# Attention, gated MLP and soft mixture in one kernel: h of three batches turned on VectorE, probabilities of two batches divided on GpSimd

## The chip, the cores and the metric

One core of a Trainium2 chip runs the whole program. The metric is device microseconds of one execution, and the median of three runs is 853.25 us (852.73 to 855.25). The profiled execution took 852.55 us.

## The reference

```
q_n = q / sqrt(mean(q*q) + 1e-6) * g_q           # k the same; 4 batches, 12 heads, 448 tokens, 64 wide
p   = exp(s - max(s)),  s = q_n @ k_n.T / 8
x   = (p / (sum(p) + 1e-9)) @ v                  # 1792 tokens x 768
h   = silu(x @ w_gate) * (x @ w_val)             # 1792 x 1536
y   = h @ w_out
logits = y @ phi                                 # 1792 x 32 slots
d = softmax of logits over all tokens;  slot_in = d.T @ y
8 experts, 4 slots each: slot_out = relu(slot_in @ w1) @ w2
out = softmax of logits over the slots @ slot_out
```

Everything is f32. `y` is never formed: the kernel uses `w_out @ phi` for the logits and `(d.T @ h) @ w_out` for the slots' input.

## The kernel before

The order of every engine's instructions is written out by hand. The program is a row of steps `t`; in each, a list of two-letter items is called one after the other, and every engine works its own instructions off in that order. `ORD1` (line 1244) is the list while the first batch's MLP runs, `ORD2` (line 1247) the list after it. Step `u = t - 28` does one 128-row half of the MLP: even `u` the gate, odd `u` the value of one block of 128 hidden units (`gv`, 18 matmuls in two halves `G0` and `G1`). A batch takes 24 steps, so batch b runs in steps 24b to 24b+23, and there are 96.

Attention runs ahead of the MLP in the same steps, one block of 112 queries for a pair of heads per step, four steps (c = 0 to 3) to a pair, pairs 7 to 23 in steps u = 0 to 67; from step 68 on there is no attention left. For each step: `S` scores on TensorE, `M0` and `M1` the row maxima on VectorE (line 473), `E0` and `E1` the exponentials with their row sums on ScalarE (line 483), `P0` and `P1` the transposes of the step before's probabilities on TensorE (line 519), `V0` and `V1` their evacuation. Once in a pair come `T` (transposes of the next pair's q in c = 0, k in c = 1), `TH` and `L` (their split in high and low parts on ScalarE and VectorE, lines 404, 434, 62, 446), `X` (probabilities times v, c = 1, line 547) and `XH`, `XL` (the split of the result, lines 59 and 62).

The division by the row sums is done once for a pair, after `X`. `NA` (line 491 on ScalarE, 492 on VectorE, 494 on GpSimd) inverts the sums and spreads them over a 112 x 512 tile, `NB` turns that tile on TensorE (line 504), `NC` evacuates it (line 511), and `XM` (line 575) multiplies.

`h` comes out of the MLP with hidden units on partitions. `AT` (tanh, line 621) and `AM` (lines 628 and 634 on VectorE) finish it, `LG` multiplies it with `w_out @ phi` for the logits (every 8 steps, in the last batch every 4, line 668). `HT` turns it to tokens on partitions: four TensorE transposes of 128 x 112 into one PSUM bank (line 647) and one ScalarE copy into `hn` (line 648), every second step. The slots' part of a batch is done in the first steps of the next: `Z1` and `Z2` in step 1, `Z3` and `Z4` in step 2, where `Z4` (line 735) reads the batch's three `hn` tiles. The pool of `hn` has three buffers.

`WH` and `WL` split the next step's weights (line 231 on ScalarE, 239 on VectorE); in the last batch `W4` does it. `G0` of the next step needs both. Short transposes and sums share the three PSUM banks of tag `t`. `Q` is the normalisation of later q and k on GpSimd (lines 340, 341 and 347).

Of the kernel before, what the change touches and what calls it, by code (L numbers as in the profile page):

```python
# [8 lines left out]
F32 = mybir.dt.float32  # L9
# [6 lines left out]
ALU = mybir.AluOpType  # L16
# [5 lines left out]
def attn_moe_softmoe_kernel(  # L22
# [33 lines left out]
    EPS_SUM = 1e-9  # L56
# [28 lines left out]
    ident = cpool.tile([P, P], F32, name="ident")  # L85
# [69 lines left out]
    NU = 2 * KF  # L155
# [126 lines left out]
    NPR = len(pairs)  # L282
    NT_ = NPR * NC
    st = {}
    xt = {}
# [191 lines left out]
    def sexp(t, j):  # L477
# [7 lines left out]
        )  # L485
        d["pr"][j] = p

    def sums_inv(i):

        su = st[i]["su"].rearrange("p c j -> p (c j)")  # L490
        nc.scalar.activation(out=su, in_=su, func=AF.Copy, bias=EPS_SUM)
        nc.vector.reciprocal(out=su, in_=su)  # L492
        rs = ap_.tile([P, 2 * NC * HD], F32, tag="rs", name="rs", bufs=1)
        nc.gpsimd.tensor_copy(  # L494
            out=rs[:CP].rearrange("p (n d) -> p n d", d=HD), in_=su.unsqueeze(2).to_broadcast([CP, 2 * NC, HD])
        )
        st[i]["rs"] = rs
# [26 lines left out]
    def pevac(t, j):  # L524
        i, c = divmod(t, NC)
        if c == 0:
            if i < NP and i % 2:
                pt = hnp.tile([CP, NC, 512], F32, tag="hn", name="pt", bufs=3)[:, :, :S]
            else:
                pt = ap_.tile([CP, NC, S], F32, tag="pt", name="pt", bufs=PTB)  # L530
            st[i].setdefault("pt", {})[j] = pt
        eng = nc.vector.tensor_copy if t < M0 and (t % 4, j) in PVD else nc.scalar.copy
        eng(  # L533
            out=st[i]["pt"][j][:, :, c * CP : (c + 1) * CP],
            in_=st[i][c]["tp", j][:CP, :S].rearrange("p (k q) -> p k q", k=NC),
        )
# [30 lines left out]
    def pv_scale(i):  # L567

        b, hp = pairs[i]
        d = st.pop(i)  # L570
        if b == 3 and hp > 3:
            xf = xfp.tile([P, S], F32, tag=f"xh{hp - 4}", name="xf", bufs=1)
        else:
            xf = d["rs"]
        nc.vector.tensor_tensor(out=xf, in0=d["xp"][:, :S], in1=d["rs"], op=ALU.mult)
        xt[b, hp] = xf
# [3 lines left out]
    bt = {}  # L580
# [49 lines left out]
    def act_val(u):  # L630
# [2 lines left out]
        ht = d["ht"][r // 2]  # L633
        nc.vector.scalar_tensor_tensor(out=ht, in0=ht, scalar=0.5, in1=d[r], op0=ALU.mult, op1=ALU.mult)

    def h_trans(u, ht=None):

        b, r = divmod(u, NU)
        fc = r // 2
        g, f4 = divmod(fc, 4)  # L640
        d = bt[b]
        if f4 == 0:
            d["hn"][g] = hnp.tile([CP, NC, 512], F32, tag="hn", name="hn", bufs=3)
        ht = d["ht"][fc] if ht is None else ht
        th4 = pt_tile("th4")
        for c in range(NC):
            nc.tensor.transpose(th4[:CP, P * c : P * c + P], ht[:, CP * c : CP * c + CP], ident)  # L647
        nc.scalar.copy(  # L648
            out=d["hn"][g][:, :, P * f4 : P * f4 + P], in_=th4[:CP, :].rearrange("p (c f) -> p c f", c=NC)
        )  # L650
# [70 lines left out]
    def slots3(b):  # L721
        d = bt[b]
        dp = pt_tile("dp")
        for c in range(NC):
            nc.tensor.transpose(
                dp[:CP, NS * c : NS * c + NS], d["et"][:NS, CP * c : CP * c + CP], ident[:NS, :NS]
            )
        d["dn"] = mp.tile([CP, NC, NS], F32, tag="dn", name="dn", bufs=1)
        nc.vector.tensor_copy(out=d["dn"], in_=dp[:CP, : NC * NS].rearrange("p (c s) -> p c s", c=NC))

    def slots4_mul(b, g):
        d = bt[b]
        sp = pt_tile("sp")
        for c in range(NC):
            nc.tensor.matmul(
                sp[NS * c : NS * c + NS, :], d["dn"][:, c, :], d["hn"][g][:, c, :], start=True, stop=True
            )
        return sp

# [167 lines left out]
    M0 = NP * NC + 4  # L907
# [150 lines left out]
    def step(t):  # L1058
        if t < M0:
            return step0(t)  # L1060
        i, c = divmod(t, NC)
        u = t - M0
        moe = u < B * NU
        prev = u - 1 if 0 <= u - 1 < B * NU else None
        ub, ur = divmod(u, NU)
        pb = ub - 1
        att = t < NT_
# [155 lines left out]
        def Q_():  # L1223
# [114 lines left out]
    with tc.manual_schedule():  # L1338
# [63 lines left out]
        for u, (e, i, n) in enumerate(eunits):  # L1402
            w = wtile.pop(u)
            if i == 0:
                if n == 0:
                    hacc[e] = s_tile(e % 3)[:, :FQ]
                for c in range(KD2 * n, KD2 * n + KD2):
                    for j in range(4):
# [4 lines left out]
                            start=(c == 0),  # L1413
                            stop=(c == KD - 1),
                        )
                if n == 1:
# [8 lines left out]
                    for t in range(2):  # L1425
                        nc.vector.tensor_copy(
                            out=h1m.rearrange("p (j t) s -> p t j s", t=2)[:, t, :, SPE * e : SPE * e + SPE],
                            in_=ht_[:, P * t : P * t + P].rearrange("p (j s) -> p j s", j=4)[
                                :, :, SPE * e : SPE * e + SPE
                            ],  # L1430
                        )
                    h1s[e] = h1m
            else:
                for kh_ in range(KH2 * n, KH2 * n + KH2) if i == 1 else range(KH):
                    for j in range(4) if i == 1 else (2 * n, 2 * n + 1):
# [4 lines left out]
                            start=(e == 0 and kh_ == 0),  # L1440
                            stop=(e == E - 1 and kh_ == KH - 1),
# [52 lines left out]
```

## Time and profile before

| | |
|---|---|
| median of 3 runs | 853.25 us |
| profiled execution | 852.55 us, of it the span 850.2 us |
| PE busy | 801.2 us (94%), 5504 matmuls |
| DVE busy | 492.1 us (58%), 785 instructions |
| ACT busy | 487.2 us (57%) |
| POOL busy | 270.0 us (32%) |

Busy time is the time in which at least one instruction of the engine ran. Matmuls overlap in the array, so that a matmul's own duration (0.37 us for 448 columns) is longer than the distance from one start to the next (0.20 us); where a step's length is told below, it is by starts. The profile's granted TensorE clock is 1.00, which is the 2.4 GHz level, in all stretches between 124 and 730 us.

### The profile page before, as it was taken

Reading aid. Unit: us, or ns where it says so; the run is one execution under the profiler, and the core shown is the slowest. Engines: PE = TensorE matmul, PEld = TensorE weight load, DVE = VectorE, ACT = ScalarE, POOL = GpSimd, SP = SyncE. Lnnn points to the kernel's source line nnn. Section 1 sums busy time; section 2 is a strip of 40 time slices with the busy share of each in tenths; the row PEclk is TensorE's granted clock in tenths of the full one; section 3 lists DMA queues with packets and bytes.
Section 4 is the critical chain, followed back from the end, with each engine's and each line's share of the span. In section 5 each row is a group of like instructions: output and inputs, shape, how many; then the busy total and the mean of one; then the engine's idle time right before and its main releaser. Section 6 shows DMA issues by size and latency. Waiting matters only on the chain.

```text
span 850.2 us, 14278 instructions
## 1 busy us (share of the span) xinstructions
PE 801.2 (94%) x5504; PEld 612.8 (72%) x5504; DVE 492.1 (58%) x785; ACT 487.2 (57%) x1054; POOL 270.0 (32%) x211
## 2 busy tenths in 40 slices
PE   6899989999999999999999999999999999988685
PEld 5566657878877767788778678877888888655343
DVE  4899888889888556565646655554354434221013
ACT  4777877889877746676667467664532323211012
POOL 7977748676777023113330230200000000010000
PEclk8999999999999999999999999999999999999877
DMA  7666655576564322322132122221227888799997
GB/s 212 201 178 205 205 179 185 178 248 198 186 196 152 108 60 66 107 89 89 51 94 89 49 78 67 86 67 57 59 77 239 294 293 319 271 383 403 403 350 235
DMA packets 77891, 148.87 MB, mean 175 GB/s; under 512 B 5888, under 2 KB 48128, under 8 KB 77824
## 3 DMA queue, kind: packets, MB, share of 16 engines
q1 hardware_dynamic: 77824, 147.97, 52.5%
q8 instruction: 43, 0.70, 0.3%
q14 instruction: 24, 0.20, 0.1%
HBM read 128.29 MB, written 19.66 MB: 174 GB/s over the span
## 4 chain that ended last, share of the span: by engine, by line
PE 76%; DVE 8%; DMA 7%; POOL 3%; ACT 3%; issue 2%; SPq 0%; POOLq 0%; ACTq 0%; DVEq 0%
PE pg L607 36%; PE tp L519 7%; PE xp L547 6%; DMA w<-in_moe_w_dram 6%; PE s L466 3%; PE s L468 3%; PE th L647 2%; PE tq L372 2%; DVE sm L473 2%; PE s L547 2%; DVE qa L434 2%; PE so L1436 2%; PE s L463 2%; PE lp L668 2%; POOL rs L494 2%
## 5 line engine op out<-in xcount | busy, mean ns | idle before, releaser
L607 PE MATMUL pg<-xh,wh 128*128 128x448 f32 x576 | 219.6, 381 | 0.0
L607 PE MATMUL pg<-xl,wh 128*128 128x448 f32 x576 | 210.3, 365 | 0.0
L607 PE MATMUL pg<-xh,wl 128*128 128x448 f32 x432 | 158.1, 366 | 0.7 <-DVE wl L239 0.7
L473 DVE TENSOR_REDUCE sm<-s 112x1 f32<-112x448 f32 x192 | 110.7, 618 | 66.6 <-PE s L468 65.3
L483 ACT ACTIVATE pr<-s,sm 112x448 f32<-112x448 f32 x192 | 121.1, 635 | 37.5 <-DVE sm L473 36.3
L494 POOL COPY rs<-su 112x512 f32<-112x512 f32 x24 | 35.6, 1484 | 275.1 <-DVE su L492 268.2
L607 PEld LDWEIGHTS pg<-xh,wh 128*128 128x128 f32 x576 | 108.4, 188 | 17.9 <-issue 10.2
L607 PEld LDWEIGHTS pg<-xl,wh 128*128 128x128 f32 x576 | 108.6, 189 | 7.0
L519 PE MATMUL tp<-ident,pr 112*112 112x112 f32 x768 | 99.6, 261 | 3.0 <-ACT wot L253 1.1
L519 PEld LDWEIGHTS tp<-ident,pr 112*112 112x112 f32 x768 | 82.2, 134 | 17.9 <-issue 2.1
L231 ACT CAST wh<-raw 128x768 fp32r<-128x768 f32 x96 | 79.7, 831 | 25.2 <-PE pg L607 21.8
L533 ACT COPY pt<-tp 112x448 f32<-112x448 f32 x164 | 81.0, 539 | 13.8 <-PE tp L519 7.8
L607 PEld LDWEIGHTS pg<-xh,wl 128*128 128x128 f32 x432 | 81.1, 188 | 8.5 <-DVE wl L239 2.0
L239 DVE TENSOR_TENSOR wl<-raw,wh 128x768 fp32r<-128x768 f32 x72 | 72.7, 1009 | 23.4 <-ACT wh L231 23.1
L341 POOL TENSOR_TENSOR ri<-ss,mhalf 112x16 f32<-112x16 f32 (+1 forms) x25 | 70.2, 2806 | 2.1
L347 POOL TENSOR_TENSOR qn<-qk,ri 112x512 f32<-112x512 f32 x46 | 62.1, 1361 | 2.3
L621 ACT ACTIVATE ht<-pg 128x448 f32<-128x448 f32 x48 | 25.9, 539 | 56.3 <-PE pg L607 56.3
L547 PE MATMUL xp<-pt,vt 112*64 112x448 f32 x288 | 58.1, 545 | 0.0
L648 ACT COPY hn<-th 112x512 f32<-112x512 f32 x48 | 28.4, 592 | 46.6 <-PE th L647 45.2
L607 PE MATMUL pg<-xh,raw 128*128 128x448 f32 x144 | 52.7, 366 | 0.0
L197 POOL TENSOR_SCALAR hpos<-r 128x768 uint16<-128x768 int16 x36 | 44.6, 1239 | 12.2 <-DVE raw L212 8.8
L628 DVE SCALAR_TENSOR_TENSOR ht<-ht,pg 128x448 f32<-128x448 f32 x48 | 29.5, 614 | 31.9 <-ACT ht L621 31.3
(160 smaller groups left out, 1208.7 us busy)
## 6 DMA issues: line engine op xcount, KB each, us to landing
w<-in_moe_w_dram SPq DMA_DIRECT2D x25, 1536.0 KB, 10.3
raw<-w SPq DMA_DIRECT2D x72, 384.0 KB, 3.1
w<-raw SPq DMA_DIRECT2D x36, 384.0 KB, 3.0
r<-in_moe_w_out_dram SPq DMA_DIRECT2D x12, 768.0 KB, 5.2
r<-in_moe_w_gate_dram SPq DMA_DIRECT2D x12, 768.0 KB, 5.7
r<-in_moe_w_val_dram SPq DMA_DIRECT2D x12, 768.0 KB, 5.3
qk<-in_q_dram SPq DMA_DIRECT2D x24, 224.0 KB, 3.4
qk<-in_k_dram SPq DMA_DIRECT2D x24, 224.0 KB, 3.5
```

What stands on the lines that cost most here:

```text
L197: (nc.gpsimd if e == "p" else nc.vector).tensor_scalar(out=o, in0=src, scalar1=-float((0x3800, 0xB800)[j]), scalar2=8.0, op0=ALU.add, op1= ...
L231: (nc.vector.tensor_copy if u - NO < NU and WH1 == "v" else nc.scalar.copy)(out=wh, in_=wst[u]["raw"])
L239: eng.tensor_tensor(out=wl, in0=wst[u]["raw"], in1=wst[u]["wh"].bitcast(F32), op=ALU.subtract)
L341: nc.gpsimd.tensor_tensor(out=ri, in0=ss, in1=mhalf[:, : len(ns)], op=ALU.pow)
L347: eng.tensor_tensor(out=st[i]["qn"][:, n].rearrange("p c h d -> p h c d"), in0=st[i]["qk"][:, n], in1=st[i]["ri"][:, n] .rearrange("p (h c ...
L473: nc.vector.tensor_reduce(out=d["sm"][:, j : j + 1], in_=d["sc"][j], axis=AX.X, op=ALU.max, negate=True)
L483: nc.scalar.activation(out=p, in_=d["sc"][j], func=AF.Exp, bias=d["sm"][:, j : j + 1], accum_out=st[i]["su"][:, c, j : j + 1])
L494: nc.gpsimd.tensor_copy(out=rs[:CP].rearrange("p (n d) -> p n d", d=HD), in_=su.unsqueeze(2).to_broadcast([CP, 2 * NC, HD]))
L519: nc.tensor.transpose(tp[:CP, ck * CP : (ck + 1) * CP], pr[:, ck * CP : (ck + 1) * CP], ident[:CP, :CP])
L533: eng(out=st[i]["pt"][j][:, :, c * CP : (c + 1) * CP], in_=st[i][c]["tp", j][:CP, :S].rearrange("p (k q) -> p k q", k=NC),)
L547: nc.tensor.matmul(xp[HD * j : HD * j + HD, :S], d["vt"][:, j, ck, :], d["pt"][j][:, ck, :], start=(ck == 0), stop=(ck == NC - 1),)
L607: nc.tensor.matmul(d[r], wt[:, P * c : P * c + P], mv, start=(c == 0 and n == 0), stop=(c == KD - 1 and n == 2),)
```

## The change

1. Batches 1 to 3: `HT` is no longer called (but for the very last block). In its place VectorE turns `h` in squares of 32 x 32, sixteen instructions for a block: item `H0` to `H3`, each four instructions over one quarter of the hidden units. A block's `H0` and `H1` stand in the step after it is finished, `H2` and `H3` in the one after that. Tokens then lie in chunks of 128, 128, 128 and 64, and `slots3` and `slots4_mul` follow that.
2. Pairs 12 to 23 (batches 2 and 3): `NA`, `NB`, `NC` and the multiplication in `XM` are gone. `N0` adds the 1e-9 and inverts two sums on VectorE, `N1` and `N2` multiply the two tiles of probabilities in place on GpSimd, in every step, before `P0` and `P1` of the next. `XH` and `XL` read the product from PSUM; two pairs of the last batch get a ScalarE copy.
3. `ORD1` gets the new items, `ORD2` is another order.

```diff
+    def normp(t, part):
+        i, c = divmod(t, NC)
+        su = st[i]["su"][:, c]
+        if part == 0:
+            nc.vector.tensor_scalar(out=su, in0=su, scalar1=EPS_SUM, scalar2=None, op0=ALU.add)
+            nc.vector.reciprocal(out=su, in_=su)
+        else:
+            j = part - 1
+            p = st[i][c]["pr"][j]
+            nc.gpsimd.tensor_scalar(out=p, in0=p, scalar1=su[:, j : j + 1], scalar2=1.0, op0=ALU.mult, op1=ALU.mult)
...
+        if i >= NPX:
+            xt[b, hp] = d["xp"][:, :S]
+            if b == 3 and hp > 3:
...
+                nc.scalar.copy(out=xf, in_=xt[b, hp])
...
+    SQ, WIDE = 32, 1
+    def h_squares(u, g):
+        hn, o = hn_tile(u)
+        hk = hts_[u][SQ * g : SQ * g + SQ]
+        for k in range(P // SQ):
+            m = (S // SQ - k + P // SQ - 1) // (P // SQ)
+            nc.vector.transpose(
+                out=hn[SQ * k : SQ * k + SQ, :m, o + SQ * g : o + SQ * g + SQ],
+                in_=hk.rearrange("p (c q) -> p c q", q=SQ)[:, k :: P // SQ],
+            )
...
-            if c == 0 and NP < i <= NPR:
+            if c == 0 and NP < i <= NPX:
                 sums_inv(i - 1)
...
-                else:
+                elif prev < NU:
                     h_trans(prev)
+        def H_(g):
+            w = prev if g < 2 else u - 2
+            if w is not None and NU <= w < B * NU - 1 and w % 2 == 1:
+                if g == 0:
+                    hts_[w] = bt[w // NU]["ht"][w % NU // 2]
+                h_squares(w, g)
...
     ORD1 = (
-        "SP X NB T S AT W4 NC XM TH XH M1 M0 Z1 P1 Z2 WH AM G0 Z3 P0 E1 XL L NA R0 CT V0 V1 SS WL G1 E0 Q HT Z4 LG R C"
+        "SP X NB T S AT W4 NC XM TH XH M1 M0 Z1 P1 Z2 WH AM G0 Z3 P0 E1 XL L NA R0 CT V0 V1 SS WL G1 E0 N0 N1 N2 Q HT H0 H1 H2 H3 Z4 LG R C"
     ).split()
     ORD2 = (
-        "AT NB X NC T S XM TH XH M0 M1 AM XL E0 E1 SP W4 G0 L NA Z1 Z3 WH P0 V0 P1 V1 Z2 Z4 HT LG SS R0 CT C WL G1 R Q"
+        "NB T TH S X M0 H2 NC NA W4 AT SP XM XH M1 AM SS E0 XL E1 N0 Z3 L P0 G0 Z1 N1 V0 HT H3 WH H0 P1 H1 N2 V1 R0 Z4 CT C WL G1 R Z2 Q LG"
     ).split()
```

## Rows read from the trace of the kernel before

**Rows 1.** The page's part 1: busy us, share of the span, instructions.
```profile
PE 801.2 (94%) x5504; PEld 612.8 (72%) x5504; DVE 492.1 (58%) x785; ACT 487.2 (57%) x1054; POOL 270.0 (32%) x211
```

**Rows 2.** Windows (busy us of PE, PEld, DVE, ACT, POOL): steps 25-47, 48-67, 72-95.
```profile
301.00:461.00 160.00, 156.64 (x932) 128.34 (x931) 93.80 (x150) 107.52 (x235) 36.84 (x27) 1.00 0.26 81
461.00:604.00 143.00, 140.08 (x833) 112.59 (x832) 78.95 (x128) 88.91 (x201) 22.00 (x17) 1.00 0.21 65
624.00:730.00 106.00, 105.62 (x551) 89.12 (x549) 46.03 (x64) 33.44 (x52) 0.29 (x1) 1.00 0.72 253
```

**Rows 3.** Waits of PE from 289 to 604 us: total, times, longest.
```profile
PE th L647 <- DVE qa L434: 4.7, 10, 0.5
```

**Rows 4.** Timeline of PE at a pair's change: start, us, instruction.
```profile
326.25 0.55 PE L519 MATMUL tp<-ident,pr 112*112 112x112 f32 x4
327.27 0.62 PE L647 MATMUL th<-ident,ht 128*112 128x128 f32 x4 [0.47 <-DVE qa L434]
...
329.36 0.36 PE L607 MATMUL pg<-xh,wl 128*128 128x448 f32 x1
329.83 0.60 PE L504 MATMUL rb<-ident,rs 112*128 112x112 f32 x4
330.36 3.23 PE L547 MATMUL xp<-pt,vt 112*64 112x448 f32 x16
```

**Rows 5.** Timeline of PE around one turned block of h, batch 3.
```profile
656.59 0.37 PE L607 MATMUL pg<-xh,raw 128*128 128x448 f32 x1
656.79 0.60 PE L647 MATMUL th<-ident,ht 128*112 128x128 f32 x4
657.15 0.45 PE L607 MATMUL pg<-xh,wh 128*128 128x448 f32 x1
657.43 0.36 PE L607 MATMUL pg<-xl,wh 128*128 128x448 f32 x1
```

**Rows 6.** Timeline of DVE in a step with c = 1.
```profile
334.76 1.16 DVE L473 TENSOR_REDUCE sm<-s 112x1 f32<-112x448 f32 x2 [0.43 <-PE s L468]
...
336.37 0.62 DVE L62 TENSOR_TENSOR xl<-rs,xh 128x448 fp32r<-128x448 f32 x1
336.90 0.61 DVE L62 TENSOR_TENSOR kl<-tq,ka 64x448 fp32r<-64x448 f32 x1
337.53 0.39 DVE L446 CAST ka<-ka 64x448 fp32r<-64x448 f32 x1
337.93 0.63 DVE L62 TENSOR_TENSOR kl<-tq,ka 64x448 fp32r<-64x448 f32 x1
338.58 0.96 DVE L239 TENSOR_TENSOR wl<-raw,wh 128x768 fp32r<-128x768 f32 x1
```

**Rows 7.** Groups of DVE by line and shape, 301 to 604 us: busy, mean ns.
```profile
L575 DVE TENSOR_TENSOR rs<-xp,rs 128x448 f32<-128x448 f32 x10 | 6.2, 625 | 37.8 <-PE xp L547 37.8
...
L492 DVE RECIPROCAL su<-su 112x8 f32<-112x8 f32 x10 | 2.0, 203 | 0.8 <-ACT su L491 0.5
...
L729 DVE COPY dn<-dp 112x128 f32<-112x128 f32 x2 | 0.6, 292 | 1.4 <-PE dp L725 1.4
```

**Rows 8.** Timelines of POOL: the spreading copy twice, and one of batch 0.
```profile
327.49 2.29 POOL L494 COPY rs<-su 112x512 f32<-112x512 f32 x1 [24.73 <-DVE su L492]
...
354.76 0.61 POOL L494 COPY rs<-su 112x512 f32<-112x512 f32 x1 [19.59 <-DVE su L492]
...
256.67 1.67 POOL L197 TENSOR_SCALAR hpos<-r 128x768 uint16<-128x768 int16 x1
```

**Rows 9.** Timeline of DVE beside the last row.
```profile
257.33 1.76 DVE L239 TENSOR_TENSOR wl<-raw,wh 128x768 fp32r<-128x768 f32 x1
```

**Rows 10.** Timelines of DVE and ACT in a step with c = 2.
```profile
340.00 1.16 DVE L473 TENSOR_REDUCE sm<-s 112x1 f32<-112x448 f32 x2 [0.46 <-PE s L468]
341.08 0.61 DVE L634 SCALAR_TENSOR_TENSOR ht<-ht,pg 128x448 f32<-128x448 f32 x1
...
341.81 0.20 ACT L483 ACTIVATION_READ_ACCUMULATOR pr<-s,sm 112x1 f32 x1
```

More of the change, by code (lines that the diff above doesn't have):

```diff
@@ L377, in attn_moe_softmoe_kernel @@
     SPL = 7
+    NPX = 2 * NP
     halves = [slice(0, HD), slice(HD, P)]
@@ L527, in pevac @@
             if i < NP and i % 2:
-                pt = hnp.tile([CP, NC, 512], F32, tag="hn", name="pt", bufs=3)[:, :, :S]
+                pt = hnp.tile([P, NC, 512], F32, tag="hn", name="pt", bufs=3)[:CP, :, :S]
             else:
@@ L570, in pv_scale @@
         d = st.pop(i)
+        if i >= NPX:
+            xt[b, hp] = d["xp"][:, :S]
+            if b == 3 and hp > 3:
+                xf = xfp.tile([P, S], F32, tag=f"xh{hp - 4}", name="xf", bufs=1)
+                nc.scalar.copy(out=xf, in_=xt[b, hp])
+                xt[b, hp] = xf
+            return
         if b == 3 and hp > 3:
@@ L634, in act_val, with tok, hn_tile @@
         nc.vector.scalar_tensor_tensor(out=ht, in0=ht, scalar=0.5, in1=d[r], op0=ALU.mult, op1=ALU.mult)
+    def tok(b):
+        return [P] * (S // P) + [S % P] if b >= WIDE else [CP] * NC
+    def hn_tile(u):
+        b, r = divmod(u, NU)
+        g, f4 = divmod(r // 2, 4)
+        d = bt[b]
+        if g not in d["hn"]:
+            d["hn"][g] = hnp.tile([P, NC, 512], F32, tag="hn", name="hn", bufs=3)
+        return d["hn"][g], P * f4
     def h_trans(u, ht=None):
         b, r = divmod(u, NU)
[L639 to L644, printed above, removed]
-        th4 = pt_tile("th4")
[L646 to L650, printed above, removed]
+        hn, o = hn_tile(u)
+        ht = bt[b]["ht"][r // 2] if ht is None else ht
+        th4 = pt_tile("th4")
+        t0 = 0
+        for c, n in enumerate(tok(b)):
+            nc.tensor.transpose(th4[:n, P * c : P * c + P], ht[:, t0 : t0 + n], ident)
+            t0 += n
+        th4 = th4.rearrange("p (c f) -> p c f", c=NC)
+        n, m = (P, NC - 1) if b >= WIDE else (CP, NC)
+        nc.scalar.copy(out=hn[:n, :m, o : o + P], in_=th4[:n, :m])
+        if b >= WIDE:
+            n = S % P
+            nc.scalar.copy(out=hn[:n, m, o : o + P], in_=th4[:n, m])
+    SQ, WIDE = 32, 1
+    def h_squares(u, g):
+        hn, o = hn_tile(u)
+        hk = hts_[u][SQ * g : SQ * g + SQ]
[5 more added lines that the diff above has]
+            )
+        if g == P // SQ - 1:
+            del hts_[u]
+    hts_ = {}
     def logits(u):
@@ L723, in slots3 @@
         dp = pt_tile("dp")
[L724 to L729, printed above, removed]
+        t0 = 0
+        for c, n in enumerate(tok(b)):
+            nc.tensor.transpose(dp[:n, NS * c : NS * c + NS], d["et"][:NS, t0 : t0 + n], ident[:NS, :NS])
+            t0 += n
+        d["dn"] = mp.tile([P, NC, NS], F32, tag="dn", name="dn", bufs=1)
+        dp = dp.rearrange("p (c s) -> p c s", s=NS)
+        n, m = (P, NC - 1) if b >= WIDE else (CP, NC)
+        nc.vector.tensor_copy(out=d["dn"][:n, :m], in_=dp[:n, :m])
+        if b >= WIDE:
+            n = S % P
+            nc.vector.tensor_copy(out=d["dn"][:n, m], in_=dp[:n, m])
     def slots4_mul(b, g):
@@ L733, in slots4_mul @@
         sp = pt_tile("sp")
-        for c in range(NC):
+        for c, n in enumerate(tok(b)):
             nc.tensor.matmul(
-                sp[NS * c : NS * c + NS, :], d["dn"][:, c, :], d["hn"][g][:, c, :], start=True, stop=True
+                sp[NS * c : NS * c + NS, :], d["dn"][:n, c, :], d["hn"][g][:n, c, :], start=True, stop=True
             )
@@ L1072, in NA @@
         def NA():
-            if c == 0 and NP < i <= NPR:
+            if c == 0 and NP < i <= NPX:
                 sums_inv(i - 1)
         def NB():
-            if c == 1 and NP < i <= NPR:
+            if c == 1 and NP < i <= NPX:
                 sums_spread(i - 1)
         def NC_():
-            if c == 1 and NP < i <= NPR:
+            if c == 1 and NP < i <= NPX:
                 sums_evac(i - 1)
@@ L1172, in E_, with NP_ @@
                 sexp(t, j)
+        def NP_(part):
+            if att and i >= NPX:
+                normp(t, part)
         def P_(j):
@@ L1229, in step @@
             E0=lambda: E_(0), E1=lambda: E_(1), P0=lambda: P_(0), P1=lambda: P_(1), V0=lambda: V_(0), V1=lambda: V_(1),
-            SP=SP, R0=R0, R=R_, CT=CT, C=C_, SS=SS, HT=HT, LG=LG, Q=Q_,
+            N0=lambda: NP_(0), N1=lambda: NP_(1), N2=lambda: NP_(2), SP=SP, R0=R0, R=R_, CT=CT, C=C_, SS=SS,
+            HT=HT, H0=lambda: H_(0), H1=lambda: H_(1), H2=lambda: H_(2), H3=lambda: H_(3), LG=LG, Q=Q_,
         )
```

## The prediction

> **What bounds the kernel now.** The page's busy times come first: PE is busy for 94% of the span, DVE for 58% [rows 1]. The windows then give the stretches that the change touches: from 301 to 604 us (steps 25 to 67, MLP and attention together) PE is busy for 296.7 of 303 us and DVE for 172.8, or 57%; from 624 to 730 us (the last batch, MLP alone) PE for 105.6 of 106 and DVE for 46.0 [rows 2]. So PE sets the pace, and VectorE has 130 and 60 us to spare. What the little idle time of PE hides is read from starts in the timeline: in a step with c = 0 the four transposes of `P1` begin at 326.25, and `th` follows after 1.02 us, where the four of `rb` let the next matmul start after 0.53: 0.5 us late, and the trace calls 0.47 idle, ended by VectorE's split of q, which frees the PSUM bank [rows 4]. PE waits there ten times, 4.7 us [rows 3].
>
> **What TensorE gains.** A turned block of `h` (four transposes) puts `th` 0.36 us ahead of the next matmul, and the one behind it comes 0.28 instead of 0.20 us later [rows 5]: 0.44 us. 35 blocks leave: 15.4 us, of it 9.2 in the 21 of the stretch 301 to 604 and 5.3 in 12 of the last one. `rb` takes 0.53 us to the start of `xp`, and starts 0.27 us late, because GpSimd's copy comes late (matmuls before it go every 0.20 us) [rows 4]. Twelve go, ten of them in 301 to 604: 5.3 us and five late starts, 1.3 us. The ten waits of 0.5 us lose their cause, nine in that stretch: 4.5 us. In 301 to 604 PE then needs 303 - 9.2 - 5.3 - 1.3 - 4.5 = 282.7 us, in the last stretch 106 - 5.3 = 100.7.
>
> **What VectorE pays.** No row shows a VectorE transpose. The nearest row is a copy of 128 elements a partition, 292 ns; the 448-element instruction with 625 ns gives (625 - 292) / 320 = 1.04 ns an element [rows 7], so 259 ns for 96 elements. Whether the next may start early is in rows 6: `xl` and the first `kl` write from partition 0 on, and the second starts 0.53 us after the first, which takes 0.62; from that `kl` to the cast the written block of partitions changes, and 0.63 us pass for an instruction of 0.61. Each of a block's sixteen transposes writes another 32 partitions than the one before, so I count them in full with 15 ns between: 8 x 0.307 + 8 x 0.274 = 4.65 us a block, 0.29 us each. From below: an early start saves 0.08 us each as with `xl`, 0.21 us; from above: two cycles an element, 0.43 and 0.37 us, worked out from the same slope; no row of this kind behaves so, and I take 0.34 us as the end of the range's price. 21 blocks are 97.6 us, 12 are 55.8.
>
> The Trainium skill, VectorE: DVE Perf Modes, section The three transpose paths, speaks against the change: its table has 311 ns for VectorE's 128 x 128 (in 32 x 32 blocks), and its rules send a whole 128 x 128 transpose to TensorE where PSUM will do as its place. No row here shows it. With 19 ns more for each of 560 transposes the sum would be 10.6 us higher, near 852.
>
> `N0` is two instructions on two columns; a reciprocal of 8 columns has 203 ns [rows 7], so 0.4 us at most, in 43 steps 17.2 us. Gone are ten or eleven multiplications `XM` and the reciprocals of eight sums: 6.2 + 0.6 + 2.0 = 8.8 us [rows 7]. In 301 to 604 VectorE then has 172.8 - 8.8 + 97.6 + 17.2 = 278.8 us.
>
> `N0` also waits: the second row sum is read out at 342.01, 2.0 us after the maxima began; VectorE comes there at 341.69 [rows 10]. That is 0.35 us with c = 2, and as much with c = 3, where `H2` delays `M1`; with c = 0 and 1 other work fills it. Over 43 steps 8 us. Queued behind `N0` are `L`, the squares and `WL`, and `G0` of the next step waits for `WL`. `H0` of steps 26, 50 and 74 overwrites an `hn` buffer that `Z4` of the same step still reads, so VectorE stands until TensorE has done `G0` and `P1`: about 1 us each. So 278.8 + 8 + 2 = 289 us for VectorE against 282.7 for TensorE.
>
> **GpSimd.** The spreading copy of 512 elements takes 0.61 us alone and 2.29 us beside VectorE [rows 8]; 448 elements then take 0.5 to 2.0 us, two of them 1 to 4 us. I take 1.6. `N0` ends 2.4 us into a step and `P0` of the next begins over 5 us into it, so neither is late. The other way about costs more: `WL` took 1.76 instead of 0.96 us beside a GpSimd instruction [rows 6, 8, 9]. At most 0.8 us x 43 = 34 us, at least nothing; in a step with c = 2 the multiplications should be over before `WL` starts. I take one `WL` in eleven, 3 us.
>
> **The rest.** ScalarE loses 35 evacuations and twelve `rs` copies and stays under VectorE. `T` ahead of `X` lets `S` and the maxima start 3.2 us earlier with c = 1; `LG` and `Z2` go to the end of the step, where only the next `WL` or the slots wait. No DMA moves. In `ORD1`, `E0` stands behind `V1`, so in steps 21 to 23 the divided tile can come late for `P1`: 0 to 4 us, I take 1.
>
> **The sum.** Two queues so nearly equal, each in its fixed order, hold each other up; I add 3 us for that, the least sure term: 289 + 3 + 3 = 295 instead of 303, 8 us less. Last stretch: VectorE 46.0 + 55.8 + 1 = 102.8, TensorE 100.7; 103.2 with little to spare, 2.8 less. Steps 24 and 68 to 71: 1.2 and 1.4 less. `ORD1` 1 more. 852.55 - 8 - 2.8 - 1.2 - 1.4 + 1 = 840.2, and the median of the runs lies 0.7 us over the profiled one: 841 us. VectorE would be the engine that sets the pace, just ahead of TensorE.
>
> **Rivals.**
> 1. Cheap transposes. At 0.21 us the 560 cost 45 us less, VectorE has slack everywhere and TensorE keeps its gain: 15.4 + 12 x 0.53 + 1.3 + 5.0 = 28.1 us less, 1 more for `ORD1`: 852.55 - 28.1 + 1 + 0.7 = 826 us. For: the maxima and `xl` do start early. Against: the blocks of partitions [rows 6].
> 2. Dear transposes, the slower side. VectorE's queue in steps 26 to 95 decides: each 10 ns on a transpose is 5.6 us, so from 0.312 us on the 12 us are gone. At 0.33 us it is 841 + 22 = 863 us. For: 32 x 32 squares may take time to fill that a copy does not; VectorE has 289 of 295 us filled. Against: nothing but the copy's row.
> 3. No net change: a new wait in place of the one removed. With c = 1, `T`, `X` and `P0` take the three banks, and `P1` needs the one that `L` frees. From the maxima to the end of `L` it is 3.8 us [rows 6], with `H2` (1.2) and `N0` (0.8) 5.8 us; TensorE is at `P1` after `X`, `P0` and `G0`, 3.2 + 0.4 + 1.8 = 5.4 us. If the late VectorE makes that 2.4 us and 1 us of it reaches the next maxima, eleven pairs cost 11 us: 852. That the change does not divide or turn at all can't be; both are written out.
>
> **Chances.** 0.3% of 853.25 is 2.6 us, about what a measurement can tell from no change. Forecast (833 to 849) 0.45; rival 1 (824 to 833) 0.18; rival 3 and the page's price (849 to 856) 0.15, of it 0.02 below 850.7; rival 2 (over 856) 0.22. So faster 0.65, same 0.12, slower 0.23. The range leaves out a little of rival 1 and half of rival 2: 825 to 860; the forecast's own is 833 to 849.
>
> **What would show it.** 560 transposes into `hn` with a mean of 0.26 to 0.29 us and starts 0.29 us apart: right; 0.21 us apart is rival 1, 0.32 rival 2. DVE at about 650 us busy. PE with 188 transposes less, and no `th` waiting for `qa`; `WL` before `G0` as PE's commonest wait, then VectorE sets the pace; `tp` waiting for `kl` is rival 3. `WL` groups with a mean over 1.1 us would show GpSimd in the way, `tp` waiting for GpSimd a division that comes late. If PE has no waits and the time is still 850, the price of its own work was misread.

## The result and the profile after

The changed kernel takes 862.66 us (median of 6 runs, 858.09 to 863.77) against 853.07 us for the kernel before beside it: a ratio of 1.0102, 95% interval 1.0074 to 1.0130. It is 1% slower, where 841 us was forecast. The profiled execution took 858.09 us; the accounting below goes by it and by the 852.55 us of the kernel before.

The busy times, part 1 of the changed kernel's page (busy us, share, instructions), answer to [rows 1]:

```profile
PE 799.7 (93%) x5316; PEld 587.0 (69%) x5316; DVE 657.8 (77%) x1420; ACT 464.8 (54%) x998; POOL 320.6 (37%) x295
```

PE has 188 matmuls less and yet no less busy time; DVE has 166 us more. The windows of the steps of [rows 2] (25 to 47, 48 to 67, and 72 to 95 from 3 us into step 72 on; busy us of PE, PEld, DVE, ACT, POOL):

```profile
303.80:464.20 160.40, 154.60 (x874) 119.71 (x873) 146.94 (x358) 98.04 (x212) 64.38 (x70) 1.00 0.25 78
464.20:606.60 142.40, 138.31 (x762) 102.92 (x762) 127.07 (x319) 81.17 (x180) 43.78 (x53) 1.00 0.22 69
629.30:734.40 105.10, 102.08 (x487) 80.21 (x485) 96.18 (x253) 25.17 (x37) 0.29 (x1) 1.00 0.72 257
```

In the first two VectorE is busy for 274 of 302.8 us, and PE now has idle time. VectorE's dearest groups there, by line and shape (busy us, mean ns, idle before), beside [rows 7]:

```profile
L694 DVE STREAM_TRANSPOSE hn<-ht 32x128 f32<-32x128 f32 x168 | 50.4, 300 | 6.7 <-PE sp L791 3.8
...
L694 DVE STREAM_TRANSPOSE hn<-ht 32x96 f32<-32x96 f32 x168 | 45.6, 271 | 2.3
L239 DVE TENSOR_TENSOR wl<-raw,wh 128x768 fp32r<-128x768 f32 x42 | 40.9, 973 | 1.3
...
L496 DVE RECIPROCAL su<-su 112x2 f32<-112x2 f32 x43 | 7.1, 166 | 1.5
L495 DVE TENSOR_SCALAR su<-su 112x2 f32<-112x2 f32 x43 | 7.0, 164 | 9.8 <-ACT pr L485 9.8
```

The transposes cost 300 and 271 ns, `N0` costs 0.33 us, and `WL` stays at 0.97 us on the mean. The forecast had 292 and 259 ns for the transposes, 0.4 us for `N0`, and a slower `WL` now and then: the prices came out within a few per cent of it, or lower. VectorE's waits in the stretch (total us, times, longest):

```profile
DVE su L495 <- ACT pr L485: 9.8, 26, 1.7
DVE hn L694 <- PE sp L791: 3.8, 2, 2.2
DVE sm L475 <- PE s L470: 3.2, 3, 1.4
DVE xl L62 <- ACT xh L59: 1.7, 1, 1.7
```

The lengths of the steps, from one step's first gate matmul to the next one's, say where the time went (us; "after 95" goes from the last gate matmul's end to ScalarE's last instruction; steps 0 to 19 take 135.7 us in both; the last column is the run e6 below, in which VectorE has little to do):

| steps | before | after | forecast | measured | e6 |
|---|---|---|---|---|---|
| up to 0 | 124.5 | 125.3 | 0 | +0.8 | 125.7 |
| 20 to 23 | 30.0 | 32.6 | +1 | +2.6 | 34.2 |
| 24 | 11.5 | 10.5 | -1.2 | -1.0 | 10.5 |
| 25 to 67 without 49, 50 | 285.6 | 282.5 | -8 with 49, 50 | -3.1 | 265.8 |
| 49, 50 | 17.0 | 20.3 | (in the row above) | +3.3 | 19.0 |
| 68 to 71 | 20.1 | 19.5 | -1.4 | -0.6 | 18.6 |
| 72 to 74 | 18.2 | 22.2 | -2.8 with 75 to 95 | +4.1 | 20.5 |
| 75 to 95 | 87.7 | 86.1 | (in the row above) | -1.6 | 84.7 |
| after 95 | 112.4 | 113.9 | 0 | +1.5 | 113.8 |

The 34.2 us of e6 in steps 20 to 23 hold a stretch at a lower granted clock, 0.79 on the mean from 279 to 287 us, where the kernels before and after have 1.00 (2.4 GHz). Two losses stand out: the slots' steps (49, 50, 73, 74 and the tail), for which the forecast had only VectorE's 1 us at the `hn` buffer, and a gain of 3 instead of 8 us in the long stretch.

Step 50 holds the first of the two. These are the groups of PE by shape while `Z4` runs, in the kernel before (484.6 to 487.5 us) and in the changed one (485.3 to 491.2 us); an f32 matmul leaves two records, so 24 are 12 matmuls:

```profile
L735 PE MATMUL sp<-hn,dn 112*32 112x512 f32 x24 | 2.8, 596 | 0.0
```

```profile
L791 PE MATMUL sp<-hn,dn 128*32 128x512 f32 x18 | 3.2, 604 | 0.0
L791 PE MATMUL sp<-hn,dn 64*32 64x512 f32 x6 | 3.1, 601 | 0.0
```

One record takes as long as before (0.60 us), but before four of them ran beside each other, each in its own 32 columns of the array; the second records of the four followed 0.45 us later, and the next four matmuls 0.88 us after the first. Now the three of 128 rows start together, their second records 0.45 us later, the one of 64 rows 0.53 us after those, its second record 0.45 us later, and the next three 0.52 us after that. It runs beside none of them: four matmuls take 1.96 us instead of 0.88, and the product 5.9 instead of 2.8. The Trainium skill, TensorEngine Tiling (Array Packing), section Key Properties, states this rule: to change the tiling mode, and not just the tile, drains TensorE. By it a 64-row matmul in between costs two drains a group; the trace agrees in that nothing runs beside it, with 1.96 us for four matmuls instead of 0.88. The forecast did not weigh it.

### The profile page after: what moved, and what is told of

The parts are those of the page before. It is cut to its first block, busy times and chain, and to the rows that moved or that the text cites. A ratio compares the mean times of both kernels' runs of the same rounds, so it can differ in the third digit from the quotient of the medians.

```text
span 856.3 us, 14739 instructions
## 1 busy us (share of the span) xinstructions
PE 799.7 (93%) x5316; PEld 587.0 (69%) x5316; DVE 657.8 (77%) x1420; ACT 464.8 (54%) x998; POOL 320.6 (37%) x295
## 5 line engine op out<-in xcount | busy, mean ns | idle before, releaser
L628 PE MATMUL pg<-xh,wh 128*128 128x448 f32 x576 | 223.9, 389 | 1.2 <-DVE ht L649 1.2
L694 DVE STREAM_TRANSPOSE hn<-ht 32x128 f32<-32x128 f32 (+1 forms) x560 | 160.1, 286 | 14.6 <-PE sp L791 5.9
L628 PE MATMUL pg<-xh,wl 128*128 128x448 f32 x432 | 161.0, 373 | 3.8 <-DVE wl L239 3.2
L500 POOL TENSOR_SCALAR pr<-pr,su 112x448 f32<-112x448 f32 x96 | 63.0, 669 | 216.2 <-DVE su L496 101.1
L475 DVE TENSOR_REDUCE sm<-s 112x1 f32<-112x448 f32 x192 | 112.4, 617 | 13.5 <-PE s L470 11.1
L533 PE MATMUL tp<-ident,pr 112*112 112x112 f32 x768 | 108.1, 263 | 10.2 <-DVE su L495 5.3
L533 PEld LDWEIGHTS tp<-ident,pr 112*112 112x112 f32 x768 | 84.2, 135 | 39.2 <-issue 18.5
L547 ACT COPY pt<-tp 112x448 f32<-112x448 f32 x164 | 85.4, 536 | 16.9 <-PE tp L533 10.4
L347 POOL TENSOR_TENSOR qn<-qk,ri 112x512 f32<-112x512 f32 x46 | 68.8, 1496 | 1.5
L468 PE MATMUL s<-ka,qa 128*112 128x448 f32 x136 | 42.2, 389 | 1.4 <-ACT pr L485 1.3
```

The lines of the kernel that those rows point to most:

```text
L347: eng.tensor_tensor(out=st[i]["qn"][:, n].rearrange("p c h d -> p h c d"), in0=st[i]["qk"][:, n], in1=st[i]["ri"][:, n] .rearrange("p (h c ...
L475: nc.vector.tensor_reduce(out=d["sm"][:, j : j + 1], in_=d["sc"][j], axis=AX.X, op=ALU.max, negate=True)
L500: nc.gpsimd.tensor_scalar(out=p, in0=p, scalar1=su[:, j : j + 1], scalar2=1.0, op0=ALU.mult, op1=ALU.mult)
L533: nc.tensor.transpose(tp[:CP, ck * CP : (ck + 1) * CP], pr[:, ck * CP : (ck + 1) * CP], ident[:CP, :CP])
L547: eng(out=st[i]["pt"][j][:, :, c * CP : (c + 1) * CP], in_=st[i][c]["tp", j][:CP, :S].rearrange("p (k q) -> p k q", k=NC),)
L628: nc.tensor.matmul(d[r], wt[:, P * c : P * c + P], mv, start=(c == 0 and n == 0), stop=(c == KD - 1 and n == 2),)
```

## The experiments

Ratios are to the kernel before, with 95% intervals.

**e1_order and e2_div: the other two parts alone.** All `h` on TensorE in 112-token chunks as before; `e1_order` also without the division on GpSimd.

```diff
-    SQ, WIDE = 32, 1
+    SQ, WIDE = 32, B
...
-                elif prev < NU:
+                else:
                     h_trans(prev)
...
-            if w is not None and NU <= w < B * NU - 1 and w % 2 == 1:
+            if False:
...
-    NPX = 2 * NP              # e1_order alone
+    NPX = NPR
```

> The changed order alone: h on TensorE and the division once a pair, as before. Theory A (VectorE, filled by the squares, sets the pace; steps 50 and 74 lose 2 us each because the first squares wait for the slots' product): no squares, so no loss, 850 to 855 us. Rival B (the division on GpSimd costs: the wait for the row sums, a late tile for the next transposes): no division here, 850 to 855. Rival C (the order itself costs: P0 ahead of G0, the logits and the softmax at the end of a step): 858 or more.

> Division on GpSimd and the changed order, h on TensorE. A: TensorE sets the pace and saves the twelve turned tiles of sums (6 us) and their late starts (1 us), and pays 2 us in steps 21 to 23: 846 to 850 us. B: 858 or more. C: about e1 less 5.

Measured: `e1_order` 854.11 us, 1.0017 (1.0002 to 1.0032); `e2_div` 850.72 us, 0.9979 (0.9962 to 0.9996). The order is worth nothing or a little less in the whole, and the division on GpSimd gains 3.4 us on top of it: four steps take 26.0 and 27.0 us, 26.6 and 27.6 with the order alone, 27.3 and 28.0 before. So the squares lose what the division gains and 9 us more.

The order's nothing is a gain and a loss. In `e1_order` steps 25 to 67 without 49 and 50 are 4.3 us shorter than before (281.3 against 285.6), and steps 75 to 95 are 6.2 us longer (93.9 against 87.7), in `e2_div` as well. There the transposes of `h` now wait for VectorE's multiplication, of which the kernel before shows nothing; PE's wait in `e2_div` from 618 to 731 us (total, times, longest):

```profile
PE th L677 <- DVE ht L655: 4.2, 10, 0.4
```

**e3_squares: the squares without the division.**

```diff
-    NPX = 2 * NP
+    NPX = NPR
```

> Squares on VectorE and the changed order, division once a pair as before. A: a pair costs VectorE 27.4 - 1.5 (two small instructions a step) - 0.8 (their waits) + 0.8 (the multiplication) = 25.9 us, about what TensorE needs with the turned sums (26.2), and steps 50 and 74 still lose 2 us each: 848 to 855 us. B: the division was the loss, 840 to 846. C: 858 or more.

Measured: 873.28 us, 1.0231 (1.0205 to 1.0257), above what A or B would have; C, the order, is ruled out by `e1_order`. Rival 3 of the forecast, a PSUM bank that VectorE frees late, is real here, at `X` instead of `P1`. The timeline of PE in step 32 (start, us, instruction, idle before):

```profile
357.40 0.60 PE L518 MATMUL rb<-ident,rs 112*128 112x112 f32 x4
357.84 0.59 PE L372 MATMUL tq<-ident,qn 112*128 112x112 f32 x4
358.20 0.64 PE L468 MATMUL s<-ka,qa 128*112 128x448 f32 x2
358.68 0.58 PE L470 MATMUL s<-kl,qa 128*112 128x448 f32 x2
362.29 4.92 PE L561 MATMUL xp<-pt,vt 112*64 112x448 f32 x16 [3.03 <-DVE lg L722]
```

`xp` waits 3 us for the bank of the logits, which VectorE reads behind its squares, and the granted clock falls from 1.00 (2.4 GHz) towards its lower level of 1.2 GHz: its mean is 0.63 from 363.5 to 367.3 us, and the 16 matmuls take 4.92 us where they take 3.23 in [rows 4]. There are four such waits from 302.8 to 622 us, 12.2 us together. Without `rb` the changed kernel has a bank more, and `xp` doesn't wait in it; `P1` does, as told below.

**e4_z4_first: `H0` and `H1` behind `Z4`**, so that VectorE doesn't stand at the `hn` buffer ahead of other work.

```diff
-"... H3 WH H0 P1 H1 N2 V1 R0 Z4 CT ..."
+"... H3 WH P1 N2 V1 R0 Z4 H0 H1 CT ..."
```

> The changed kernel with H0 and H1 behind Z4, so that VectorE evacuates the slots' products before it begins the squares that wait for them. A: steps 50 and 74 give back most of 2.3 us each, 856 to 860 us where the changed kernel has 862.7, and other steps stay as they are. B and C: no change, 861 to 864.

Measured: 861.97 us, 1.0106 (1.0087 to 1.0126), and step 50 takes 11.369 us as in the changed kernel. VectorE's wait for the buffer is not what lengthens it; this led to the shapes of `sp` above.

**e5_pad128: no matmul of 64 rows.**

```diff
+            if b >= WIDE:
+                nc.vector.memset(d["hn"][g][S % P :, NC - 1], 0.0)
...
+            nc.vector.memset(d["dn"][n:, m], 0.0)
...
-                sp[NS * c : NS * c + NS, :], d["dn"][:n, c, :], d["hn"][g][:n, c, :], start=True, stop=True
+                sp[NS * c : NS * c + NS, :],
+                d["dn"][: P if b >= WIDE else n, c, :],
+                d["hn"][g][: P if b >= WIDE else n, c, :],
+                start=True,
+                stop=True,
```

> The changed kernel with the fourth token chunk of batches 1 to 3 filled up with zeros to 128 rows (VectorE clears 64 rows of hn's fourth chunk once a tile, and of dn's once a batch), so that no matmul of the slots' product has 64 rows. Theory A (the 64-row matmul can't run beside the three of 128 rows: in step 50 the six of 64 rows are busy for 3.1 us by themselves, the eighteen of 128 rows for 3.2): the 24 matmuls take 2.7 us again as in the kernel before, steps 50 and 74 are 3 us shorter (11.37 to about 8.4 us, 10.08 or 11.37 to about 7.2), the tail as well; in all 853 to 855 us. Theory B (the matmuls wait for hn or dn, or for a PSUM bank that VectorE frees late): they stay near 5.9 us and the time near 862 us.

Measured: 859.93 us, 1.0083 (1.0060 to 1.0105). PE's group and the added VectorE instruction:

```profile
L794 PE MATMUL sp<-hn,dn 128*32 128x512 f32 x24 | 3.0, 596 | 0.0
```

```profile
L668 DVE MEMSET hn<- 64x512 f32 x1 | 0.5, 485 | 0.2 <-issue 0.2
```

The product is back at 3.0 us, step 50 at 8.37 instead of 11.37, step 74 at 8.2 instead of 10.1, the tail at 112.3 instead of 113.9: theory A holds for the product, and the time misses its 853 to 855 us. Of these 6.5 us only 2.7 remain between the medians: every eighth step from 27 to 91, where the memset stands, became 0.6 to 1.0 us longer (step 35 from 6.13 to 6.86), 6.6 us in the nine steps. In the profiled runs nothing remains (860.19 against 858.09 us); there `e5_pad128` also has a mean granted clock of 0.79 from 279 to 287 us, where the changed kernel has 1.00, and takes 1.6 us more in steps 20 to 23. The steps pay for 0.49 us of added work on VectorE with the whole of it and some more: what is put into its queue at that place lengthens the step.

**e6_two_instr: VectorE relieved.** Two instructions over all 128 partitions turn a block. Each square stays in its 32 partitions, so `h` does not get to the places that the slots' product reads, and the result is not the reference's: the run serves to price VectorE's queue alone.

```diff
-        for k in range(P // SQ):
-            m = (S // SQ - k + P // SQ - 1) // (P // SQ)
-            nc.vector.transpose(
...
+        if g == 0:
+            nc.vector.transpose(out=hn[:, : NC - 1, o : o + P], in_=ht[:, : S - S % P].rearrange("p (c q) -> p c q", q=P))
+            nc.vector.transpose(out=hn[:, NC - 1, o : o + P], in_=ht[:, S - P :])
```

> The changed kernel with a block of h turned by two VectorE instructions over all 128 partitions (squares turned in place, so h stands in the wrong places for the slots' product) instead of sixteen over 32 partitions. 35 blocks, each about 0.6 us instead of 4.65 (estimate: 448 + 64 columns at 1.04 ns and two overheads). Theory A (outside the slots' steps VectorE's queue sets the pace of the changed kernel: 27.6 us for four steps): four steps take 25.5 to 26 us, TensorE's own work, steps 49 and 73 lose their 1 and 2.3 us, the slots' matmuls stay at 5.9 us; in all 833 to 842 us. Rival (GpSimd's division or ScalarE's chain sets the pace, VectorE's waits only move): four steps stay above 27 us, the time above 855.

Measured: 837.49 us, 0.9817 (0.9791 to 0.9844): 25 us less than the changed kernel, though it still has the 64-row matmuls. VectorE's groups from 303.8 to 594 us, and two windows, which here hold about steps 25 to 48 and 49 to 67 (with 2 us of step 24 and 3 us of step 68):

```profile
L693 DVE STREAM_TRANSPOSE hn<-ht 128x384 f32<-128x384 f32 x22 | 12.5, 568 | 4.5 <-PE sp L788 4.2
L694 DVE STREAM_TRANSPOSE hn<-ht 128x128 f32<-128x128 f32 x22 | 5.9, 269 | 0.0
```

```profile
303.80:464.20 160.40, 160.16 (x936) 127.71 (x934) 112.97 (x220) 103.35 (x225) 74.19 (x72) 1.00 0.28 86
464.20:594.00 129.80, 129.56 (x734) 101.92 (x731) 83.65 (x168) 76.06 (x170) 50.39 (x50) 1.00 0.22 69
```

PE is busy throughout again, four steps take 25.1 and 26.2 us, and steps 49 and 73 come back to 7.6 and 5.8 us from 9.0 and 7.5. (5.8 is also what step 73 takes in `e1_order` and `e2_div`, 0.5 more than before: that much is the order's.) So VectorE's queue sets the changed kernel's pace, in the long stretch and in the slots' chain of step 73.

**e7_in_place: squares turned in place, and a product of the slots that reads them there**, so that the result is the reference's.

```diff
+        nc.vector.transpose(out=hall[:, r // 2], in_=hts_.pop(u) if ht is None else ht)
...
+        nc.vector.transpose(out=d["dn"], in_=d["et"])
...
+        for k in range(S // SQ):
+            for a in range(P // SQ):
+                q = slice(SQ * a, SQ * a + SQ)
+                nc.tensor.matmul(
+                    sp[q, : KF * SQ],
+                    d["dn"][q, SQ * k : SQ * k + SQ],
+                    hall[q, :, SQ * k : SQ * k + SQ],
+                    start=(k == 0),
+                    stop=(k == S // SQ - 1),
+                )
```

> A version made from the two theories: h of all four batches turned in place, one VectorE instruction of 128 x 448 a block; the exponentials (which stand four times on the partitions) turned in place by one instruction too, instead of dp; the slots' product as 14 x 4 matmuls of 32 rows, 32 columns and 384 elements, four beside each other on the diagonal, summed over the tokens in one PSUM bank; the slots' input turned for the output product by VectorE squares, so the twelve small matmuls of the tail go. If VectorE's sixteen instructions and the slots' product were what the change lost on: four steps at 25.5 to 26 us, batch 0 loses 12 x 0.44 = 5 us of TensorE, the product takes 14 x 0.32 = 4.5 us (0.43 us for four of 512 elements in the kernel before, 0.32 for 384): 826 to 836 us. If four 32-row matmuls don't run beside each other, the product takes 4 x 4.5 = 18 us in each of four batches, and the time is 870 or more.

Measured: 852.49 us, 0.9991 (0.9976 to 1.0005). The stretch is TensorE's (25.1 and 26.2 us for four steps), but the product takes 9.2 us, twice the estimate:

```profile
L749 PE MATMUL sp<-hall,dn 32*32 32x384 f32 x112 | 9.2, 482 | 0.6 <-DVE dn L741 0.6
```

Four do run beside each other, 0.32 us a group as estimated; there are 28 groups of records and not 14, because an f32 matmul leaves two. Steps 26, 50 and 74 and the tail grow by 4 to 8 us each beside the changed kernel, which takes the whole gain.

**e8_half, e9_half_npx, e10_half_swapped: half of the blocks back to TensorE** in batches 1 and 2, with the padded chunk. `on_pe` names the blocks that `HT` turns. `e10_half_swapped` differs from `e9_half_npx` in two things: the other half of the blocks, and GpSimd instead of VectorE clears the 64 rows.

```diff
+    def on_pe(w):
+        return w < NU or (w < last_att and w // 2 % 2 == 1)          # e10: == 0
+
+    last_att = (B - 1) * NU
...
+                nc.vector.memset(d["hn"][g][S % P :, NC - 1], 0.0)   # e10: nc.gpsimd
...
-    NPX = 2 * NP              # e9 and e10
+    NPX = 2 * NP + 1
```

> The changed kernel with the padded fourth chunk of e5_pad128, and with every other block of h of batches 1 and 2 (odd fc) turned on TensorE again; all blocks of batch 3 stay with VectorE. Theory A (VectorE's queue sets the pace of the changed kernel, and TensorE's own work is 25.2 and 26.2 us for four steps, as in e6_two_instr): VectorE loses 4.65 us in four steps and needs about 23, TensorE 0.44 more, so 25.6 and 26.6 us for four steps; the clearing of 64 rows, which in e5_pad128 lengthened seven steps by 0.7 us each, is hidden; 837.5 + 10 x 0.44 - 3 x 3 = about 833 us, 828 to 839. Rival (the two queues so near each other hold each other up, whatever VectorE has left): four steps near 27 us and 843 us or more.

> e8_half with the division on GpSimd from step 24 on (with ORD2) instead of step 20: the last pair under ORD1 divides by the replicated row sums as before. If the division under ORD1 is what lengthens steps 20 to 23 (by 2.6 us beside the kernel before in the changed kernel, by 0.4 in e3_squares without the division): about 2 us less than e8_half. If it is the order of ORD1 itself: no difference, or 0.5 us more for the one more pair with TensorE's replicating product.

> e9_half_npx with the halves exchanged: in batches 1 and 2 even fc goes to TensorE (its transposes fall into steps with c = 2), odd fc to VectorE's squares (steps with c = 0 and 1); GpSimd instead of VectorE clears the 64 rows. In e8_half the steps with c = 0 took 10.6 and 11.4 us, 1.66 and 1.48 more than in e6_two_instr, where 0.44 was due: H3 delayed WL and so the maxima and the exponentials of that step, and P1 waited 0.60 us for the PSUM bank that ScalarE frees behind them, beside th. Theory A (place decides, not the amount): with th in steps with c = 2, where bank and engines are free, four steps take 25.6 to 26.2 and 26.6 to 27.2 us, and the time is about 840 us (835 to 845). Rival (the two queues as near each other as this hold each other up wherever the block is): four steps stay at 27 and 28 us and the time at 853 to 856.

Measured: 854.90 us, 1.0026 (1.0010 to 1.0041); 854.40 us, 1.0008 (0.9994 to 1.0023); 846.49 us, 0.9921 (0.9899 to 0.9943). Theory A's figure for `e8_half` was missed by 22 us: four steps took 26.8 and 28.2 us, although VectorE was no longer full (busy for 233 of 301 us in steps 25 to 67, against 274 of 303 in the changed kernel). Beside `e6_two_instr` the steps with c = 0 are 14.7 us longer in that stretch, and the six steps with the clearing, which A had as hidden, 4.9. PE's waits in its steps 25 to 67 (total, times, longest):

```profile
PE tp L533 <- ACT pt L547: 5.0, 9, 0.6
PE pg L628 <- DVE wl L239: 2.6, 6, 0.7
```

`H3` ahead of `WL` delays the maxima, the exponentials and so the evacuation that frees `P1`'s bank, in just the steps where `th` takes one more: this reading of the timeline led to `e10_half_swapped`. There the steps with c = 0 are back at 8.95 and 9.96 us, as in `e6_two_instr`, so what lengthened them is gone. But the loss has moved and not gone: in steps 25 to 67 they are 14.6 us shorter than in `e9_half_npx`, and those with c = 1 and 2 are 15.2 us longer, since steps with c = 2 cost 1.1 us more than in `e6_two_instr` instead of 0.44. Between the medians 8 us are gone. In the profiled runs the nine steps where the clearing left VectorE are 6.7 us shorter (step 35 from 6.20 to 5.65), and all other steps from 25 to 94 together 0.6. So the exchange of the halves is worth next to nothing and the clearing's place nearly all of it, as far as the profiles show; the exchange alone was not run. Four steps take 26.8 and 27.4 us, where 26.2 and 27.2 were the upper ends, and the time lies between A's 835 to 845 and the rival's 853.

In `e9_half_npx` steps 20 to 23 are 3.9 us shorter than in `e8_half` and steps 24 and 25 1.6 us longer. Of the 3.9 us 1.6 are the granted clock, 0.79 on the mean from 279 to 287 us in `e8_half` and 1.00 in `e9_half_npx`. At 1.00 the four steps take 32.6 us with the division under `ORD1` (changed kernel) and 30.3 without (`e3_squares`, `e9_half_npx`), so it costs 2.3 us, and most of it comes back later; the 0.5 us between the medians lie within the intervals.

**e11_last_batch: squares where VectorE is idle**, in the last batch alone, its fourth chunk padded; the others on TensorE, the division from step 24 on.

```diff
-    SQ, WIDE = 32, 1
+    SQ, WIDE = 32, B - 1
...
+                nc.gpsimd.memset(d["hn"][g][S % P :, NC - 1], 0.0)
...
-    NPX = 2 * NP
+    NPX = 2 * NP + 1
```

> Squares only in the last batch, where no attention is left and VectorE is half idle; batches 0 to 2 turn h on TensorE and keep 112-row chunks; the last batch's fourth chunk is padded to 128 rows (cleared by GpSimd); the division on GpSimd from step 24 on. Steps 25 to 71 should be as in e2_div (26.5 us for four steps), the steps 72 to 95 as in the changed kernel (5.3 us of TensorE less than before), the tail without the 3 us of the 64-row matmuls: 850.7 - 5 - 1 = 844 to 846 us. If the last batch's gain is given back in steps 72 to 74 (VectorE's squares in the way of the slots' chain of batch 2: 2.3 us in step 73 of the changed kernel), 847 to 849.

Measured: 842.28 us, 0.9871 (0.9847 to 0.9895), better than both kernels. The windows of its steps 25 to 67, and of most of 72 to 95 with the tail's first 8 us:

```profile
304.00:597.50 293.50, 291.03 (x1721) 234.26 (x1720) 185.89 (x343) 189.88 (x412) 116.75 (x122) 1.00 0.25 76
620.00:730.00 110.00, 108.62 (x565) 86.84 (x566) 93.84 (x244) 29.61 (x49) 1.79 (x4) 1.00 0.76 272
```

PE is busy for 99% in both. Steps 75 to 95 take 86.5 us against 93.9 in `e2_div`, steps 72 to 74 17.9 us, and the tail 111.0. Most of the gain in steps 75 to 95 takes back what the new order had lost there: beside the kernel before, with its 87.7 us, the squares win 1.2. What makes this version faster than the kernel before is in steps 25 to 67 without 49 and 50, 276.2 us instead of 285.6: the order and the division. The old order in the last batch with TensorE's transposes was not tried.

## Why the prediction was wrong

**Right.** The price of the transposes (0.29 us from start to start forecast, 0.297 measured; the mean of one is 0.286), `N0`'s wait (8 forecast, 9.8 us measured), VectorE's busy time (650 and 658 us), the waits for `qa` (none left), and TensorE's own gain: 20.3 us less was forecast for 301 to 604, and `e6_two_instr` shows 19.8 less in those steps without 49 and 50. Rival 2's time came (863 us), but not by its mechanism: it needed a price of 0.33 us.

On the Trainium skill, VectorE: DVE Perf Modes, section The three transpose paths: for its 311 ns (128 x 128, in a column for bf16) the trace has 269 ns, for one instruction of 128 x 128 f32 in `e6_two_instr`. The rule on the same page of the Trainium skill, section Rules for kernel authors, to leave whole 128 x 128 transposes to TensorE where PSUM will do, fits what happened, but through the sixteen instructions that it takes here to reach other partitions, and not through the price of one.

**The step that failed first** is one that the sum does not contain. "`slots3` and `slots4_mul` follow" the new chunks, and I gave the product the cost that it had. Its 64-row matmuls add 3.1 us in each of three batches, and without them steps 50 and 74 and the tail are 3.0, 1.9 and 1.6 us shorter (`e5_pad128`).

**The second** is "I add 3 us for that, the least sure term": two queues in fixed order hold each other up. In steps 25 to 67 VectorE is busy for 274 us, as forecast (278.8 with 5 us of gaps between the transposes in it). But it waits for 19 us instead of 10, and the gaps between its 676 instructions are 10.5 us, which I counted for the transposes alone. The stretch without steps 49 and 50 gained 3.1 us; the forecast for all of it was 8.

TensorE's dearest wait in that stretch is not the one for `WL`, which the forecast named as the sign, but one of `P1`'s transposes for VectorE (PE's waits from 303.8 to 606.6 us, and the timelines of step 29):

```profile
PE tp L533 <- DVE su L495: 5.3, 8, 1.0
PE pg L628 <- DVE wl L239: 2.1, 9, 0.3
```

```profile
334.85 1.18 DVE L694 STREAM_TRANSPOSE hn<-ht 32x128 f32<-32x128 f32 x4
...
337.26 0.62 DVE L62 TENSOR_TENSOR xl<-xp,xh 128x448 fp32r<-128x448 f32 x1
337.79 0.16 DVE L495 TENSOR_SCALAR su<-su 112x2 f32<-112x2 f32 x1
...
338.02 0.57 PE L533 MATMUL tp<-ident,pr 112*112 112x112 f32 x4 [0.99 <-DVE su L495]
```

All eight are in steps with c = 1, and each starts 0.14 or 0.15 us after `xl` has read `X`'s product from PSUM, which VectorE does behind the four squares of `H2`. The profile names `su`, which ends in between and which these transposes don't read; the bank of the product is the likely cause. So rival 3's wait came, with c = 1 as named, at another bank than the one that `L` frees; the forecast's sum had nothing for it. Without steps 49 and 50, those with c = 1 are 6.7 us longer than in `e6_two_instr`, those with c = 3, 2 and 0 4.8, 2.8 and 2.4 us; with c = 2 and 3 the first gate matmul that reads `WL` starts late, by 0.5 us in step 39.

**The third** is the slots' chain in steps 49 and 73: "`LG` and `Z2` go to the end of the step, where only the next `WL` or the slots wait". The slots do wait. VectorE's timeline in step 73 of the changed kernel, and PE's:

```profile
633.82 0.96 DVE L239 TENSOR_TENSOR raw<-raw,wh 128x768 fp32r<-128x768 f32 x1
634.69 0.61 DVE L649 SCALAR_TENSOR_TENSOR ht<-ht,pg 128x448 f32<-128x448 f32 x1
635.34 1.20 DVE L694 STREAM_TRANSPOSE hn<-ht 32x128 f32<-32x128 f32 x4
636.56 0.62 DVE L756 TENSOR_REDUCE sml<-lt 128x1 f32<-128x448 f32 x1
```

```profile
638.19 0.40 PE L777 MATMUL dp<-ident,et 32*128 32x32 f32 x4 [1.67 <-ACT et L764]
```

The maximum of the slots' logits stands behind the squares, and TensorE waits for the exponentials. Step 73 is 2.3 us longer than before and step 49 1.0; `e6_two_instr` gives back 1.7 and 1.3 of it.

**The fourth** is `ORD1`, "0 to 4 us, I take 1": a size, and it was 2.6 us. In step 21 the transposes wait for GpSimd's divided tile, as named:

```profile
281.10 0.59 PE L533 MATMUL tp<-ident,pr 112*112 112x112 f32 x4 [1.54 <-POOL pr L500]
```

Of the 17.9 us between the forecast's 840.2 and the profiled 858.09 these four are 6.5, about 4 (8.2 in steps 25 to 67, less 3.0 and 1.0 that are in the first and third), 3.3 and 1.6. The other 2.5 are small differences in steps 68 to 95 and the stretch before step 0, which no part of the change touches and which varies from 124.5 to 125.8 us over all runs. **Open:** the median lies 4.6 us over the profiled run, the fastest of the six. The mean granted clock of that whole run is 0.978, and 0.968 to 0.975 in the other five. Other profiles show what a stretch at a lower clock costs. In `e4_z4_first`, profiled at 861.87 us, it is 0.84 on the mean from 640 to 651 us, right after the stalls of step 74, where the changed kernel has 1.00, and step 74, which its edit touches too, takes 11.37 us instead of 10.08. `e1_order` and `e3_squares` have the same instructions in steps 20 to 23; with a clock of 0.79 from 266 to 274 us the first takes 31.9 us, with 1.00 the second takes 30.3. By these 1.6 us, three such stretches would make up the 4.6, an estimate; whether and where they lay in the five runs was not recorded.

## What to carry to other kernels

When a change cuts tokens or rows into other chunks, go through every matmul that reads them and ask which of them ran beside each other before: one odd shape in a group of four doubled the group's time. Work given to an idle engine pays only where that engine is idle in the same steps and nothing on the other engines' path stands behind it in its queue: beside TensorE's transposes (`e2_div`, 275.4 us for steps 25 to 67 without 49 and 50) the same squares lost 7 us next to attention and gained 7 in the last batch, 6 of which the new order had lost there. Where one edit holds an order, a division and a transpose, compare each part stretch by stretch: the order's 4 us of gain and 6 of loss don't show in the total. Where two queues in fixed order come out within a few per cent of each other, as 289 and 283 us here, their sum is no forecast.

## What the hardware showed unexpectedly

- A 64-row matmul of 32 columns behind three 128-row ones: 1.96 us for the four, against 0.88 with all at 112 (kernel before) or all at 128 rows (`e5_pad128`).
- A VectorE transpose over 128 partitions costs what one over 32 partitions does: 269 ns for 128 x 128, 300 ns for 32 x 128; 128 x 448 took 634 ns. The sixteen instructions are the price that moving squares to other partitions had here.
- GpSimd multiplied 112 x 448 by a scalar for each partition in 0.66 us. Eleven of 42 `WL` ran beside such a multiplication, for 0.2 us each, and took 1.00 us on the mean; the others took 0.96. A longer overlap, as in [rows 8] and [rows 9], did not occur in these steps, so its cost stays open.
- After 3 us of idle time the 16 matmuls of `xp` took 4.92 instead of 3.23 us at a granted clock of 0.63 on the mean, 1.7 us on top of the stall.
